# Every second attention head of the last two chunks in token-major form: normalized probabilities turned by the DMA crossbar, value-stationary products

## The chip, the core and the metric

The kernel runs on one core of one Trainium2 chip. Such a core has a matrix engine (TensorE, "PE" in the profile, with its weight loads as "PEld"), VectorE (DVE), ScalarE (ACT), GpSimd (POOL), SyncE (SP, which here only issues DMAs) and 16 DMA engines. Matrix products read SBUF and write PSUM, which has eight banks of 512 float32 columns. The metric is the device time of one execution in microseconds (us); lower is better.

## What is computed

A transformer block with 2048 tokens of width 1024, whose two halves are scaled, shifted and gated by six vectors made from a condition `c` (`mod = silu(c) @ w_mod`):

```python
h = layernorm(x) * (1 + ca) + sa
q = (h @ wq).reshape(2048, 32, 128)          # 32 query heads of width 128
k, v = last 512 cached keys and values        # 4 key/value heads, each for 8 query heads
p = softmax(q @ k.T * 128 ** -0.5)            # no mask: every token sees the same 512 keys
x = x + ga * ((p @ v) @ wo)
h = layernorm(x) * (1 + cb) + sb
x = x + gb * ((silu(h @ w_gate) * (h @ w_up)) @ w_down)     # inner width 3584
```

Inputs and output are bfloat16.

## The kernel before

**Chunks and heads.** The tokens are worked in 4 chunks of 512. The attention half is one loop over `i` from 1 to 129, where head number `i` counts all 4 x 32 heads (chunk `i // 32`, head `i % 32`). The loop is a software pipeline written out by hand. Iteration `i` issues, in this order: the query projection of head `i + 3` (`qproj`, L642: eight matmuls into PSUM bank 4, then a DVE cast into one of five `qT` slots), the scores of head `i - 1` (`scores`, L805) and the value products of head `i - 2` (`pv`, L816). When a chunk's last head is through, the output projection of that chunk follows (`oproj`, L872: eight groups of 32 matmuls, in banks 4 and 7, each ended by two DVE operations of `resid`, L851). In the last chunk it is spread over the end of the loop and the code behind it. Then comes the feed-forward half, chunk by chunk: `gateup` and `down`.

**One head.** `scores` is key-major: for each of four key tiles, the keys are the stationary operand and the 512 queries move, so that banks 0 to 3 hold scores with keys on partitions. Two ACT exponentials of 1024 columns each (L813) write them, not normalized, to `ex_s`. `pv` then needs no transposition for its products: for every token tile `j` and key tile `kt` the probabilities are stationary and the values move, with a column of ones appended, 129 columns in all (16 matmuls into banks 5 and 6). The ones give the sum of each token's row. DVE takes its reciprocal (L831), multiplies (L834) and a DMA transpose (L837) turns the result to the form that the output projection needs, `oT_all`.

**Queues.** Every operation goes through one tracker (`_Tracker.op`, L62), which puts waits on semaphores ahead of it in its engine's queue; each queue runs in program order. A wait of DVE for an earlier DVE result is a wait as well. All attention DMAs are issued from SP, so a DMA whose source isn't ready holds all later ones: the `oT` transposes, the 1 MB loads of `wq` for four heads each (`load_wq`, L353), the transposes of the next layernorm (L454), and 24 transposing loads of `w_mod` columns (`load_mt`, L584), each followed by a DVE operation with an accumulated sum (`mod_col`, L592).

**Side work.** `bg` holds generators for the layernorm of the next chunk; `run_bg(1)` at the end of each iteration takes one step of it (a half of the statistics, the rest of them, the normalization with its transpose, and at the end the modulation of two tiles). It is filled at the third iteration of a chunk and lasts 19 steps. `LOADT` gives the iterations of the 24 column loads, one every 9/4 heads from iteration 34 on, and `mod_col` follows four iterations behind its load. `wq` is loaded at iterations with `i % 4 == 1`; the load for group `(i + 4) // 4 + 1` of four heads is first used by the query projection four iterations later.

**Memory.** Nearly all of SBUF is one array, `arena`, in which regions are reused by offset; a new region inherits the waits of what it overlaps (`_Arena.at`, L103). `tmp` are the two scratch tiles of `resid`.

Of the kernel before, what the change touches and what calls it, by code (L numbers as in the profile page):

```python
# [3 lines left out]
ALU = mybir.AluOpType  # L4
AF = mybir.ActivationFunctionType
BF16 = mybir.dt.bfloat16
F32 = mybir.dt.float32
P = 128
# [122 lines left out]
def bass_adaLN_cond__sliding_block_cached__swiglu_ffn__prompt_kernel(  # L131
# [27 lines left out]
    TPC = CH // P  # L159
# [3 lines left out]
    att_scale = float(Dh) ** -0.5  # L163
    eps = 1e-5
    NA = NCH * Hq
# [29 lines left out]
    rstd = [rstd4[:, i:i + 1] for i in range(4)]  # L195
    bq = S_("bq", [P, 8], F32)
    rl = [S_("rl%d" % i, [P, 4], F32) for i in range(2)]
    nsc = [S_("nsc%d" % i, [P, D], BF16) for i in range(2)]
    tmp = [S_("tmp%d" % i, [P, 512], F32) for i in range(2)]

    KB = 1024
    A_BYTES = 162 * KB
    arena_t = S_("arena", [P, A_BYTES // 2], BF16)
    arena = _Arena(arena_t[:, :], A_BYTES)
# [6 lines left out]
    OFF_H20 = 154 * KB  # L211
# [10 lines left out]
    def bank(b, n=512, off=0):  # L222
        return ps[:, b * 512 + off:b * 512 + off + n]
# [10 lines left out]
    PB = [_Buf("bank%d" % b) for b in range(8)]  # L234
# [8 lines left out]
    B_mv = [_Buf("mv%d" % i) for i in range(4)]  # L243
    B_rs = [_Buf("rs%d" % i) for i in range(4)]
    B_rl = [_Buf("rl%d" % i) for i in range(2)]
    B_ns = [_Buf("ns%d" % i) for i in range(2)]
    B_tmp = [_Buf("tmp%d" % i) for i in range(2)]
    B_h2 = [[_Buf("h2_%d_%d" % (s, dt)) for dt in range(DT)] for s in range(2)]
# [8 lines left out]
    SCB = 0  # L257
    PVB = 5
    XB = 7

    with nc.Block() as block:

        @block.gpsimd
        def _(g):
            V = nc.vector
            A = nc.scalar
            TE = nc.tensor
            SP = nc.sync

            def mm(out_ap, lhsT, rhs, start, stop, reads, bank_buf, skip=False):  # L270
                T.op(PE, lambda: TE.matmul(out_ap, lhsT, rhs, start=start, stop=stop, skip_group_check=skip),  # L271
                     reads=reads, writes=[bank_buf])
# [7 lines left out]
            def run_bg(n=1):  # L280
                while n > 0 and bg:
                    try:
                        next(bg[0])
                        n -= 1
                    except StopIteration:
                        bg.pop(0)

            def finish(gen):
                while gen in bg:
# [6 lines left out]
                 reads=[B_ident], writes=[B_ident])  # L296
# [17 lines left out]
            OFF_HT = 80 * KB  # L314
            OFF_OT = 96 * KB
            OFF_EX = 128 * KB
# [56 lines left out]
            B_va = _Buf("va")  # L373
# [254 lines left out]
            def q_slot(i):  # L628
                return NQT + i % 2 if i < NQ0 else i % NQT
# [186 lines left out]
            def pv(i):  # L816
                ch, h = divmod(i, Hq)
                gk = h // rep
                es = i % NEX
                os_ = i % NOS  # L820

                for jj in range(2):
                    for kt in range(KT):
                        for jb in range(2):
                            j = 2 * jb + jj
                            b = PVB + jb
                            mm(bank(b, P + 1, jj * 130), ex_s[es][:, kt, j * P:(j + 1) * P], v_aug[:, gk * KT + kt, 0:P + 1],
                               kt == 0, kt == KT - 1, [B_ex[es], B_va, B_vg[gk]], PB[b])
                both = [PB[PVB], PB[PVB + 1]]
                r = i % 2  # L830
                T.op(DVE, lambda: V.reciprocal(rl[r][:, :].rearrange("p (a b) -> p a b", a=2), psap(PVB * 512 + P, [[512, 2], [130, 2]])),  # L831
                     writes=both + [B_rl[r]])
                rlb = bass.AP(tensor=rl[r][:, :].tensor, offset=0, ap=[[4, P], [2, 2], [1, 2], [0, P]])
                T.op(DVE, lambda: V.tensor_tensor(o_s[os_].rearrange("p (a b) d -> p a b d", a=2),  # L834
                                                  psap(PVB * 512, [[512, 2], [130, 2], [1, P]]), rlb, ALU.mult),
                     reads=[B_rl[r]], writes=both + [B_os[os_]])
                T.op(Q_tr[os_], lambda: SP.dma_start_transpose(oT_all[:, h, :].rearrange("p (j q) -> p j q", j=TPC),  # L837
                                                               o_s[os_].rearrange("p j d -> p (j d)")),
                     reads=[B_os[os_]], writes=[B_oT[h]])

            B_wo = [_Buf("wo%d" % i) for i in range(8)]
            wo_s = [None] * 8
            Q_wo = [dq("q_wo%d" % i) for i in range(8)]
# [49 lines left out]
            GATER = {19 + n: NGP + n for n in range(DT - NGP)}  # L893
            GATET = {23: 0, 24: 1}
            GATES = {26: 0, 27: 1}
            t2 = Hq + 6 + (9 * (NL - 1)) // 4
            TURNT = (28, t2 + 1)
            PUTT = {33: (0, c_sil, B_csil), 30: (1, mrow[0:DT, :], B_mrow), t2 + 3: (2, mrow[0:DT, :], B_mrow)}
            GETT = {35: (0, sc_row, B_scr), 31: (1, rowb[0][:, :], B_row[0]), t2 + 4: (2, rowb[1][:, :], B_row[1])}
            LOADT = {Hq + 2 + (9 * n) // 4: n for n in range(NL)}  # L900
            LOADO = {5 + (21 * p) // 8: p for p in range(8)}
            LOADK = {1: 1, 5: 2, 6: 3}
            for i in range(1, NA + 2):
                ch, h = divmod(i, Hq)
                if i in LOADK:
                    load_k(LOADK[i])
                if i == 4:
                    load_wq((i + 4) // 4 + 1)
# [24 lines left out]
                if i + LEAD < NA:  # L933
                    if (i + LEAD) % Hq == 0:
                        finish(ln1[(i + LEAD) // Hq])
                    if i == 1:
                        scores(0)
                    if i in (1, 3, 5):
                        q_bias_mm(i + 1, i + 3, XB)
                    if i > NQ0:  # L940
                        qproj(i + LEAD)
                    elif i % 2 == 1:
                        qproj_mm(NQ0 + i // 2, QB, 0, HK)
                    else:
                        qproj(NQ0 - 1 + i // 2, QB, HK)
                if i - 4 in LOADT:
                    n = LOADT[i - 4]
                    mod_col(n)
                    g0, last = divmod(n, DT)
                    if last == DT - 1:  # L950
                        mod_take(g0, B_late[g0 + 1])
                        if g0 == 1:
                            mod_gain(1, B_late[2], B_g[1])
                n = i - (NA - LEAD)
                if 0 <= n <= 2:
                    oproj_mm(NCH - 1, 0, QB, 8 * n, 8 * n + 8)
                elif n >= 3:
                    oproj_mm(NCH - 1, 1, XB, 8 * (n - 3), 8 * (n - 3) + 8)
                if 1 <= i - 1 < NA:
                    scores(i - 1)  # L960
                if 0 <= i - 2 < NA:
                    pv(i - 2)
                    ch2, h2 = divmod(i - 2, Hq)
                    if i % 4 == 1 and i > 5:
                        load_wq((i + 4) // 4 + 1)
                    if i in LOADT:
                        load_mt(LOADT[i])
                    if h2 == Hq - 1 and ch2 < NCH - 1:
                        oproj(ch2)
                run_bg(1)  # L970
                for n in GATEP.get(i, ()):
                    gate_part(n)
                if i in GATER:
                    gate_row(GATER[i])
                if i in GATES:
                    gate_sum(GATES[i])
                if i == max(GATER):
                    gate_split()
# [152 lines left out]
```

## Time and profile before

| what | value |
|---|---|
| median of 3 runs | 1270.15 us (1269.91 to 1270.49) |
| the profiled execution's own time | 1270.14 us |
| its span, from the first to the last instruction | 1268.3 us |
| granted TensorE clock | 1.00 |
| attention of chunk 2 (iterations 66 to 97, from the trace) | about 361 to 472 us |
| attention of chunk 3 | about 528 to 638 us |
| busy in the stretch 359 to 470 us: PE, DVE, ACT | 110.16, 72.21, 63.43 of 111 us |
| busy in the stretch 526 to 637 us: PE, DVE, ACT | 110.16, 57.08, 63.43 of 111 us |

The span is what the trace shows; 1.8 us of the execution lie around it. A busy share of PE is the union of its matmul records, whose ends are modelled, so it tells that something was always in flight and not how fast; the pace is read from the distance between events that follow a fixed number of matmuls. SP is a queue that issues DMAs: its instruction's duration is the issue, and the data land later ("to landing", counted from the start of the issue).

### The profile page before, as it was taken

The page shows a single profiled execution, that of the slowest core. Times are in us where ns is not written, and L with a number is a line of the kernel's source. Part 1 is how long each engine was busy: PE and PEld are TensorE (multiplying, and loading weights), DVE is VectorE, ACT ScalarE, POOL GpSimd, SP SyncE. Part 2 cuts the span into 40 slices and gives each one's busy share as a digit, 9 for nine tenths or more (in the row PEclk, how much of TensorE's full clock was granted, in tenths as well). Part 3 has the DMA queues.
Part 4 walks back from the last instruction along what each step waited for, and adds up shares of the span by engine and source line. Part 5 has one row for each costly group of instructions (what it writes and reads, how often), then busy time and mean ns, then how long its engine had stood idle before and what let it go on. Part 6 is the DMA issues. An engine that isn't in the chain of part 4 may idle for free.

```text
span 1268.3 us, 17609 instructions
## 1 busy us (share of the span) xinstructions
PE 1255.1 (99%) x7442; PEld 640.7 (51%) x7583; DVE 485.1 (38%) x894; ACT 341.6 (27%) x389; POOL 56.0 (4%) x95
## 2 busy tenths in 40 slices
PE   8999999999999999999999999999999999999999
PEld 5655545555455554555544444444444444444444
DVE  4676226764257641365322321233212321222122
ACT  4655205553035550155510111011100111011100
POOL 1530000000000000000000000000000000000000
PEclk9999999999999999999999999999999999999999
DMA  9998306875029641064243972055512644034200
GB/s 320 264 263 218 92 1 127 177 171 125 1 57 177 138 114 34 9 129 123 61 145 100 291 246 94 25 158 150 168 40 72 177 141 134 17 128 154 67 9 25
DMA packets 239997, 156.67 MB, mean 124 GB/s; under 512 B 133296, under 2 KB 225840, under 8 KB 239920
## 3 DMA queue, kind: packets, MB, share of 16 engines
q1 hardware_dynamic: 181664, 96.83, 31.6%
q10 hardware_dynamic: 58256, 58.73, 14.6%
q8 instruction: 59, 0.97, 0.3%
q14 instruction: 18, 0.15, 0.1%
HBM read 119.93 MB, written 4.20 MB: 98 GB/s over the span
## 4 chain that ended last, share of the span: by engine, by line
PE 98%; issue 1%; DMA 0%; SPq 0%; DVE 0%
PE ps L271 98%; DMA arena<-in_w_mod_dram 0%; SPq L309 0%; SPq L334 0%; PE ps L275 0%; DVE arena L496 0%; DVE tmp L853 0%; DVE arena L855 0%; DVE gain_f L486 0%
## 5 line engine op out<-in xcount | busy, mean ns | idle before, releaser
L271 PE MATMUL ps<-arena 128*128 128x512 bf16 (+1 forms) x7213 | 1249.3, 333 | 10.1 <-POOL arena L298 2.0
L271 PEld LDWEIGHTS ps<-arena 128*128 128x128 bf16 x7354 | 632.9, 98 | 621.5 <-issue 2.1
L813 ACT ACTIVATE arena<-ps 128x1024 bf16<-128x1024 f32 x256 | 261.9, 1023 | 345.1 <-PE ps L271 333.4
L1059 ACT ACTIVATE arena<-ps 128x512 bf16<-128x512 f32 x112 | 66.9, 597 | 499.6 <-PE ps L271 499.6
L1060 DVE TENSOR_TENSOR arena<-ps,arena 128x512 bf16<-128x512 f32 x112 | 77.5, 692 | 276.2 <-PE ps L271 276.2
L853 DVE TENSOR_TENSOR tmp<-ps,rowb 128x512 f32<-128x512 f32 (+1 forms) x65 | 44.4, 683 | 318.8 <-PE ps L271 318.8
L644 DVE CAST arena<-ps 128x512 bf16<-128x512 f32 x120 | 82.8, 690 | 47.7 <-PE ps L271 47.7
L834 DVE TENSOR_TENSOR arena<-ps,rl 128x512 bf16<-128x512 f32 x128 | 88.5, 691 | 4.7 <-DVE rl L831 0.2
L831 DVE RECIPROCAL rl<-ps 128x4 f32<-128x4 f32 x128 | 23.4, 182 | 114.1 <-PE ps L271 114.1
L429 POOL TENSOR_SCALAR rstd<-mv 128x1 f32<-128x1 f32 x28 | 6.1, 216 | 910.3 <-DVE mv L428 910.3
L424 DVE BATCH_NORM_STATS2 st<-x_res 128x6 f32<-128x512 bf16 x62 | 42.4, 683 | 3.4 <-DMA x_res<-in_A_x_dram 3.3
L593 DVE SCALAR_TENSOR_TENSOR arena<-arena 128x1024 bf16<-128x1024 bf16 x24 | 29.2, 1215 | 0.0
L855 DVE TENSOR_TENSOR arena<-tmp,x_res 128x512 bf16<-128x512 f32 (+2 forms) x33 | 22.3, 677 | 1.1
L855 DVE TENSOR_TENSOR x_res<-tmp,x_res 128x512 bf16<-128x512 f32 x32 | 22.2, 693 | 1.1
L440 DVE TENSOR_SCALAR arena<-arena,gain,mod_bf 128x512 bf16<-128x512 bf16 x56 | 21.2, 420 | 0.0
L435 DVE TENSOR_SCALAR nsc<-x_res,mv,rstd 128x1024 bf16<-128x1024 bf16 x30 | 19.2, 641 | 0.0
L431 POOL TENSOR_TENSOR rstd<-rstd,mhalf 128x1 f32<-128x1 f32 x28 | 15.7, 559 | 2.3
L772 POOL TENSOR_SCALAR arena<-arena,sc_bf 128x512 f32<-128x512 bf16 x8 | 12.9, 1614 | 0.5 <-POOL arena L774 0.2
L774 POOL TENSOR_TENSOR arena<-arena 128x512 f32<-128x512 f32 x8 | 10.1, 1265 | 0.7
L428 DVE BATCH_NORM_AGGREGATE mv<-st 128x2 f32<-128x12 f32 x28 | 5.8, 209 | 1.0
L271 PEld LDWEIGHTS ps<-sc_bf,arena 128*128 128x128 bf16 x128 | 4.4, 96 | 1.4 <-DMA arena<-in_w_mod_dram 0.3
L271 PE MATMUL ps<-sc_bf,arena 128*128 128x1 bf16 x128 | 4.7, 164 | 0.3 <-DMA arena<-in_w_mod_dram 0.3
(56 smaller groups left out, 59.4 us busy)
## 6 DMA issues: line engine op xcount, KB each, us to landing
arena<-in_A_wq_dram SPq DMA_DIRECT2D x30, 1024.0 KB, 5.8
arena<-in_B_w_gate_dram ACTq DMA_DIRECT2D x28, 1024.0 KB, 5.4
arena<-in_B_w_up_dram ACTq DMA_DIRECT2D x28, 1024.0 KB, 7.9
arena<-in_A_wo_dram SPq DMA_DIRECT2D x8, 1024.0 KB, 7.6
arena<-in_B_w_down_dram SPq DMA_DIRECT2D x7, 1024.0 KB, 8.3
out_dram<-arena SPq DMA_DIRECT2D x15, 256.0 KB, 2.0
x_res<-in_A_x_dram SPq DMA_DIRECT2D x3, 1024.0 KB, 7.0
arena<-arena SPq DMA_TRANSPOSE x132, 2.6
```

The costliest lines, as they stand in the source:

```text
L271: T.op(PE, lambda: TE.matmul(out_ap, lhsT, rhs, start=start, stop=stop, skip_group_check=skip), reads=reads, writes=[bank_buf])
L424: T.op(DVE, lambda: V.bn_stats(st_[sl][:, hf * 6:hf * 6 + 6], x_res[:, t, hf * 512:hf * 512 + 512]), reads=[B_x[t]], writes=[B_st[sl]])
L440: T.op(DVE, lambda: V.tensor_scalar(dst[:, dt, :], dst[:, dt, :], gain[gi][:, dt:dt + 1], mod_bf[:, ccol + dt:ccol + dt + 1], op0=ALU.mult ...
L593: T.op(DVE, lambda: V.scalar_tensor_tensor(mt[n % 2], mt[n % 2], 1.0, sc_row, op0=ALU.mult, op1=ALU.mult, accum_out=mcol[:, n:n + 1]), rea ...
L644: T.op(DVE, lambda: V.tensor_copy(qT_s[qs], bank(b)), writes=[PB[b], B_qT[qs]])
L813: T.op(ACT, lambda: A.activation(ex_s[es][:, 2 * kp:2 * kp + 2, :], banks2(SCB + 2 * kp), AF.Exp, scale=att_scale), writes=[PB[SCB + 2 * k ...
L831: T.op(DVE, lambda: V.reciprocal(rl[r][:, :].rearrange("p (a b) -> p a b", a=2), psap(PVB * 512 + P, [[512, 2], [130, 2]])), writes=both + ...
L834: T.op(DVE, lambda: V.tensor_tensor(o_s[os_].rearrange("p (a b) d -> p a b d", a=2), psap(PVB * 512, [[512, 2], [130, 2], [1, P]]), rlb, A ...
L853: T.op(DVE, lambda: V.tensor_tensor(tmp[s][:, 0:n], bank(b, n), rowb[ri][:, c0:c0 + n], ALU.mult), reads=[B_row[ri]], writes=[PB[b], B_tmp ...
L855: T.op(DVE, lambda: V.tensor_tensor(dst[:, c0:c0 + n], tmp[s][:, 0:n], x_res[:, t, c0:c0 + n], ALU.add), reads=[B_tmp[s], B_x[t]], writes= ...
L1059: T.op(ACT, lambda: A.activation(sg_s[ss], bank(gb), AF.Silu), writes=[PB[gb], B_sg[ss]])
L1060: T.op(DVE, lambda: V.tensor_tensor(guT[:, ft, :], bank(ub), sg_s[ss], ALU.mult), reads=[B_sg[ss]], writes=[PB[ub], B_gu[ft]])
```

## The change

The 31 heads 66, 68, ..., 126 (`NAT`: the even ones of chunks 2 and 3, without head 64) go another way.

- **Scores token-major** (`nat_scores`): for each of four token tiles the queries are stationary and the 512 keys move, still four matmuls of 512 columns in banks 0 to 3, but with tokens on partitions. Four ACT exponentials of 512 columns, each with an accumulated row sum (`psum`), write `pn`. They are issued two iterations earlier in the count of heads than `scores` would be: in the odd iteration `i`, for head `i + 1`, between the query projection and the value products.
- **Normalization** (`nat_norm`), in two halves of two token tiles: a DVE reciprocal of two sums, then two DVE multiplications of 512 columns in place. The first half is issued in the odd iteration behind `pv(i - 2)`, the second in the next one behind its query cast.
- **Turning** (`nat_turn`): each half, 128 x 1024 values, goes through a DMA transpose of SP to `pt`, so that keys are on partitions.
- **Products** (`nat_pv`), three iterations behind the scores: four matmuls with the values stationary and 512 tokens moving, into bank 5. The result is already in the form of `oT_all`; one DVE copy puts it there, without a DMA.
- **Room.** `pn` of even slots takes the place of one `ex_s`, that of odd slots the two `tmp`; `pt` (two slots of 4 KB a partition) moves through three regions that are free at the time (`PTAT`).
- **Seams.** Where a chunk ends (iterations 65 and 97) the early scores come behind `pv`, and the two transposes behind the output projection.
- **Moved with it.** `wq` is loaded at `i % 4 == 2` from iteration 66 on, so one iteration later. The 24 column loads come every 3/2 heads instead of 9/4, `mod_col` three iterations behind its load instead of four, and the last row's turning and loading follow earlier. `run_bg(1)` comes ahead of the early scores in odd iterations.

```diff
+            NAT = set(range(2 * Hq + 2, NA, 2))
+            B_pn = [[_Buf("pn0_%d" % hf) for hf in range(2)], B_tmp]
+            pn = [[None, None], [t[:, :].bitcast(BF16) for t in tmp]]
...
+            def nat_scores(i):
...
+                for j in range(TPC):
+                    mm(bank(SCB + j), qT_s[qs][:, j * P:(j + 1) * P],
+                       kT_sb[:, gk * KT:(gk + 1) * KT, :].rearrange("p a b -> p (a b)"), True, True,
+                       [B_kT[gk], B_qT[qs]], PB[SCB + j])
+                for j in range(TPC):
+                    hf, jj = divmod(j, 2)
+                    T.op(ACT, lambda: A.activation(pn[s][hf][:, jj * 512:(jj + 1) * 512], bank(SCB + j), AF.Exp, scale=att_scale,
+                                                   accum_out=psum[s][:, j:j + 1]),
+                         writes=[PB[SCB + j], B_pn[s][hf], B_psum[s][hf]])
+
+            def nat_norm(i, hf):
+                s = p_slot(i)
+                T.op(DVE, lambda: V.reciprocal(pinv[s][:, 2 * hf:2 * hf + 2], psum[s][:, 2 * hf:2 * hf + 2]),
+                     reads=[B_psum[s][hf]], writes=[B_pinv[s][hf]])
+                for jj in range(2):
+                    j = 2 * hf + jj
+                    T.op(DVE, lambda: V.tensor_scalar(pn[s][hf][:, jj * 512:(jj + 1) * 512], pn[s][hf][:, jj * 512:(jj + 1) * 512],
+                                                      pinv[s][:, j:j + 1], None, op0=ALU.mult),
+                         reads=[B_pinv[s][hf]], writes=[B_pn[s][hf]])
+
+            def nat_turn(i, hf):
+                s = p_slot(i)
+                pt_of[i] = (pt[s], B_pt[s])
+                T.op(Q_pt[2 * s + hf], lambda: SP.dma_start_transpose(pt[s][:, 2 * KT * hf:2 * KT * (hf + 1), :], pn[s][hf]),
+                     reads=[B_pn[s][hf]], writes=[B_pt[s][hf]])
+
+            def nat_pv(i):
...
+                for kt in range(KT):
+                    mm(bank(PVB).rearrange("p (j q) -> p j q", j=TPC), v_aug[:, gk * KT + kt, 0:P], ptv[:, :, kt, :],
+                       kt == 0, kt == KT - 1, [B_va, B_vg[gk]] + pb, PB[PVB])
+                T.op(DVE, lambda: V.tensor_copy(oT_all[:, h, :], bank(PVB)), writes=[PB[PVB], B_oT[h]])
...
-            LOADT = {Hq + 2 + (9 * n) // 4: n for n in range(NL)}
+            LOADT = {Hq + 2 + (3 * n) // 2: n for n in range(NL)}
...
+            PTAT = {2 * Hq + 2: OFF_OT + 24 * KB, 2 * Hq + 16: OFF_H20, 3 * Hq: OFF_HT}
...
+                seam = (i - 1) % Hq == 0 and i + 1 in NAT
+                if i + 1 in PTAT and not seam:
+                    pt_region(PTAT[i + 1])
+                if i in NAT and (i - 2) % Hq:
+                    nat_norm(i, 1)
+                    nat_turn(i, 1)
+                nat = i % 2 == 1 and i + 1 in NAT
+                if nat and not seam:
+                    run_bg(1)
+                    nat_scores(i + 1)
-                if 1 <= i - 1 < NA:
+                if 1 <= i - 1 < NA and i - 1 not in NAT:
                     scores(i - 1)
                 if 0 <= i - 2 < NA:
-                    pv(i - 2)
+                    if i - 2 in NAT:
+                        nat_pv(i - 2)
+                    else:
+                        pv(i - 2)
+                    if nat:
+                        if seam:
+                            nat_scores(i + 1)
+                        nat_norm(i + 1, 0)
+                        if seam:
+                            nat_norm(i + 1, 1)
+                        else:
+                            nat_turn(i + 1, 0)
                     ch2, h2 = divmod(i - 2, Hq)
-                    if i % 4 == 1 and i > 5:
+                    if i % 4 == (1 if i < 2 * Hq else 2) and i > 5:
                         load_wq((i + 4) // 4 + 1)
```

More of the change, by code (lines that the diff above doesn't have):

```diff
@@ L197, in bass_adaLN_cond__sliding_block_cached__swiglu_ffn__prompt_kernel @@
     rl = [S_("rl%d" % i, [P, 4], F32) for i in range(2)]
+    psum = [S_("psum%d" % i, [P, 4], F32) for i in range(2)]
+    pinv = [S_("pinv%d" % i, [P, 4], F32) for i in range(2)]
     nsc = [S_("nsc%d" % i, [P, D], BF16) for i in range(2)]
@@ L245, in bass_adaLN_cond__sliding_block_cached__swiglu_ffn__prompt_kernel @@
     B_rl = [_Buf("rl%d" % i) for i in range(2)]
+    B_psum = [[_Buf("psum%d_%d" % (i, hf)) for hf in range(2)] for i in range(2)]
+    B_pinv = [[_Buf("pinv%d_%d" % (i, hf)) for hf in range(2)] for i in range(2)]
     B_ns = [_Buf("ns%d" % i) for i in range(2)]
@@ L839, in pv, with p_slot @@
                      reads=[B_os[os_]], writes=[B_oT[h]])
+            NAT = set(range(2 * Hq + 2, NA, 2))
+            B_pn = [[_Buf("pn0_%d" % hf) for hf in range(2)], B_tmp]
+            pn = [[None, None], [t[:, :].bitcast(BF16) for t in tmp]]
+            B_pt = [[_Buf("pt%d_%d" % (s, hf)) for hf in range(2)] for s in range(2)]
+            pt = [None, None]
+            pt_of = {}
+            Q_pt = [dq("q_pt%d" % i) for i in range(4)]
+            def p_slot(i):
+                return (i - (2 * Hq + 2)) // 2 % 2
@@ new lines, in pt_region @@
+            def pt_region(off):
+                for s in range(2):
+                    old = B_pt[s]
+                    B_pt[s] = [_Buf("pt%d_%d" % (s, hf)) for hf in range(2)]
+                    for hf in range(2):
+                        B_pt[s][hf].absorb(old[hf])
+                    pt[s] = arena.at(off + s * 4 * KB, [TPC * KT, P], BF16, B_pt[s])
+            def nat_scores(i):
+                gk = i % Hq // rep
+                qs = q_slot(i)
+                s = p_slot(i)
+                if pn[0][0] is None:
+                    for hf in range(2):
+                        pn[0][hf] = arena.at(OFF_EX + hf * 2 * KB, [2 * KT * P], BF16, [B_pn[0][hf]])
+                for j in range(TPC):
[7 more added lines that the diff above has]
+                         writes=[PB[SCB + j], B_pn[s][hf], B_psum[s][hf]])
@@ new lines, in nat_turn @@
+            def nat_turn(i, hf):
+                s = p_slot(i)
+                pt_of[i] = (pt[s], B_pt[s])
+                T.op(Q_pt[2 * s + hf], lambda: SP.dma_start_transpose(pt[s][:, 2 * KT * hf:2 * KT * (hf + 1), :], pn[s][hf]),
+                     reads=[B_pn[s][hf]], writes=[B_pt[s][hf]])
+            def nat_pv(i):
+                h = i % Hq
+                gk = h // rep
+                s = p_slot(i)
+                pa, pb = pt_of.pop(i)
+                ptv = pa.rearrange("p (j k) q -> p j k q", j=TPC)
+                for kt in range(KT):
+                    mm(bank(PVB).rearrange("p (j q) -> p j q", j=TPC), v_aug[:, gk * KT + kt, 0:P], ptv[:, :, kt, :],
+                       kt == 0, kt == KT - 1, [B_va, B_vg[gk]] + pb, PB[PVB])
+                T.op(DVE, lambda: V.tensor_copy(oT_all[:, h, :], bank(PVB)), writes=[PB[PVB], B_oT[h]])
@@ L895, in _ @@
             GATES = {26: 0, 27: 1}
-            t2 = Hq + 6 + (9 * (NL - 1)) // 4
+            t2 = Hq + 6 + (3 * (NL - 1)) // 2
             TURNT = (28, t2 + 1)
@@ L945, in _ @@
                         qproj(NQ0 - 1 + i // 2, QB, HK)
-                if i - 4 in LOADT:
-                    n = LOADT[i - 4]
+                if i - 3 in LOADT:
+                    n = LOADT[i - 3]
                     mod_col(n)
@@ L969, in _ @@
                         oproj(ch2)
-                run_bg(1)
+                        if seam:
+                            if i + 1 in PTAT:
+                                pt_region(PTAT[i + 1])
+                            for hf in range(2):
+                                nat_turn(i + 1, hf)
+                if not nat or seam:
+                    run_bg(1)
                 for n in GATEP.get(i, ()):
```

## The prediction

> **What bounds the kernel now.** I read the page first: the busy shares, then the chain that ended last, then the groups with their shapes kept apart.
>
> ```profile
> PE 1255.1 (99%) x7442; PEld 640.7 (51%) x7583; DVE 485.1 (38%) x894; ACT 341.6 (27%) x389; POOL 56.0 (4%) x95
> ...
> PE 98%; issue 1%; DMA 0%; SPq 0%; DVE 0%
> ...
> L271 PE MATMUL ps<-arena 128*128 128x512 bf16 x5085 | 1134.2, 380 | 9.5 <-POOL arena L298 2.0
> ...
> L271 PE MATMUL ps<-arena 128*128 128x129 bf16 x2048 | 137.0, 220 | 0.0
> ```
>
> PE is the path nearly everywhere, and in the attention of chunks 2 and 3 the list of waits shows none of PE. So only two things count: how many slots PE needs, and whether something new makes it wait. The matmul records overlap, so their means are no prices. I take the pace from the timeline: gate-up work first (16 matmuls of 512 columns from one SiLU on ACT, L1059, to the next), then four heads of chunk 3, then the landings of the wq loads (L357) of chunks 2 and 3.
>
> ```profile
> 700.83 0.60 ACT L1059 ACTIVATE arena<-ps 128x512 bf16<-128x512 f32 x1 [2.86 <-PE ps L271]
> 707.73 0.60 ACT L1059 ACTIVATE arena<-ps 128x512 bf16<-128x512 f32 x1 [2.86 <-PE ps L271]
> ```
> ```profile
> 547.28 2.14 ACT L813 ACTIVATE arena<-ps 128x1024 bf16<-128x1024 f32 x2 [1.36 <-PE ps L271]
> 548.62 0.18 DVE L831 RECIPROCAL rl<-ps 128x4 f32<-128x4 f32 x1 [1.08 <-PE ps L271]
> 548.84 0.69 DVE L834 TENSOR_TENSOR arena<-ps,rl 128x512 bf16<-128x512 f32 x1
> 549.44 0.54 DVE L435 TENSOR_SCALAR nsc<-x_res,mv,rstd 128x1024 bf16<-128x1024 bf16 x1
> 550.35 0.69 DVE L644 CAST arena<-ps 128x512 bf16<-128x512 f32 x1 [0.36 <-PE ps L271]
> ...
> 557.77 2.14 ACT L813 ACTIVATE arena<-ps 128x1024 bf16<-128x1024 f32 x2 [1.36 <-PE ps L271]
> 557.83 0.53 SPq L357 DMA_DIRECT2D arena<-in_A_wq_dram  x1
> ```
> ```profile
> L357 SPq DMA_DIRECT2D arena<-in_A_wq_dram x13: 506/532/535, 376.7 to 599.8; - x13
> ...
> DMA to landing us min/median/max: 5.3/5.8/7.5
> ```
>
> From 700.83 to 707.73 lie 32 matmuls: 0.2156 us each. From 547.28 to 557.77 lie three heads: 3.497 each. A head has 12 matmuls of 512 columns (2.587), so its 16 of 129 columns take 0.910, or 0.057 each. A wq load of those two chunks lands 5.3 to 7.5 us after its issue. The last matmul's record outlasts its slot by 0.16 (0.380 less 0.216), and at the kernel's end DVE starts 0.04 behind it; so an engine sees a product 0.2 after PE's slot has passed on.
>
> **The change, part by part.** *Products.* Sixteen slots (0.910) become four (0.862): 0.048 less, 31 times, **-1.5 us**. The new moving operand is read in four runs of 128 columns; no row has that. If each run paid the 0.057 of a 129-column slot, the four matmuls would take 0.912 and the gain were nothing; below 0.862 there is no row. I take 0.862, the row of the same 512 columns. The scores keep four slots.
>
> The Trainium skill ("TensorE: Matmul & The Clock Gate", section "Back-to-back issue gap") gives sustained spacings of about 81 ns at 128 columns and 131 ns at 512. By it, as an estimate, a head would save 16 x 0.081 - 4 x 0.131 = 0.77 and the change 24 us. The trace disagrees on both, 57 and 216 ns, and decides.
>
> *ACT.* Two exponentials (2.14) become four of 512 columns: 0.60 each by L1059's row, plus 0.19 for reading the accumulator (L518's row) and up to 0.09, the pause between the two of a head; 3.1 to 3.5 together. A pair of heads then has 5.3 to 5.6 of 6.95 us. It lies beside PE as long as bank 3 is free for the next scores. The odd iteration taken as zero, in times that engines see: query products 1.73, early scores 1.94 to 2.59, value products 3.50; then 5.22, scores 6.08, new products 6.95. The four exponentials run from 1.94 to 5.1 or 5.4; PE's slot for bank 3 comes at 6.08 - 0.22 - 0.2 = 5.66. Covered; if one cost 0.93 instead, the cover is gone, and each us more is paid once a pair.
>
> *DVE.* Reciprocal and multiplication (0.9) become two reciprocals (0.21 each up to the next start), four multiplications of 0.35 (L675, one scalar) to 0.41 (L440, two) and a copy of 0.69. Per pair, with two layernorm steps of about 0.75, some 6.4 of 6.95. The first half can start behind L834: 3.50 + 0.22 + 0.61 (next starts 0.60 behind it above) = 4.33, and lasts 0.21 + 0.35 + 0.04 + 0.35 = 0.95, to 5.28. The cast holds DVE to 5.89, the second half ends at 6.84 (7.07 with the dearer row). Bank 4 is free a us ahead of the next query products. Cover enough.
>
> *The turned halves.* Each is shaped like a layernorm transpose (L454: issue 1.25, landing 3.1, median 3.7, 6.2 at most in these chunks). The second goes out at 6.87 and is read at 13.03 - 0.2: 5.9 us. Hidden; only a landing near 6.2 would show. The `oT` transpose (landing 2.4 to 2.7 mostly) goes away; the copy replaces it in time.
>
> *The wq load.* This is where I see a wait. Before, SP issued it behind the odd head's `oT` transpose, 5.71 into its iteration (557.83 against 552.12), four iterations ahead of its use: 4 x 3.497 - 0.2 - 5.71 = 8.1 us for a landing of 7.5 at most. Now it stands behind the second turn, which stands behind DVE: 6.87 + 1.25 + 0.09 = 8.21, that is 4.71 into the even iteration, and three iterations ahead: 3.449 + 3.497 + 3.449 - 0.2 - 4.71 = **5.5 us**. Median landing 5.8 and a PE restart of some 0.1 make 0.4; with the dearer multiplication 0.6. Ends: nothing (5.3) and 2.0 (7.5). I take 0.45, nearest to the median, as the quiet landings (5.4 to 5.6) are of loads with fewer transposes around. Loads of iterations 74 to 94 and 102 to 118 are so placed, 11; that of 98 isn't, as SP waits for nothing at that seam. **+5.0** (0 to 22).
>
> *Start of chunk 2.* (a) In iteration 65 the early scores follow scores 64 by one `pv` (0.91): bank 2 is wanted 0.91 + 0.43 - 0.2 = 1.14 behind the end of those scores, and the second exponential ends 1.71 behind it (2.14 less 0.43): **+0.6**. Iteration 97 has no scores ahead: nothing. (b) The load for heads 72 to 75 went out ahead of the output projection; now its turn comes behind the turns of head 66, which wait for that projection's end (their room is `oT`), and behind the `oT` of head 64: 5.7 into iteration 66 by the timeline (first `oT` issue of the chunk 4.4 behind the projection's end). Left: 10.44 - 0.2 - 5.7 = 4.5 against 5.8: **+1.3** (0.8 to 3.0). (c) `mod_col` (1.21) runs in iterations 67, 68, 70 and 71, in the same queue ahead of the normalization. The load of iteration 70 is so issued 1.2 later than in a quiet pair: 0.4 + 1.2 = **+1.5** (0.5 to 3).
>
> *The other moves.* The denser column loads put 1.21 on DVE in two of three iterations of chunk 1: with cast, reciprocal, multiplication and a layernorm step 3.0 of 3.50; landings of 3.1 to 6.4 against three heads. Issue on SP (1.3 to 2.4) fits between the `oT`. Regions of `pt` are free before they are entered (last `mod_col` in 71, room entered in 79; `hT` of chunk 2 last read in 92). `tmp` under `pn` delays `resid` at seam 97 only if a turn hadn't landed in the 6.9 us of the first group. Nothing; if DVE overflowed, bank 4 would pass it on one to one.
>
> **Sum.** -1.5 + 0.6 + 1.3 + 1.5 + 5.0 = +6.9. Span 1268.3 to 1275.2; the profiled execution took 1270.14, the median of the runs shown is 1270.15, so **1277.0**.
>
> **Rivals.**
> - *The wq load is hidden* (not slower): SP gets to it early or landings stay at 5.3 to 5.5. For: five of the 13 loads land within 5.6. Against: 5.5 leaves no room, and a 256 KB turn runs just ahead. It decides at 5.4. With (b) and (c) halved by the same: -1.5 + 0.6 + 1.4 = +0.5: 1270.7.
> - *SP becomes late*: a third transpose in a row is issued slowly. For: the one at 395.59, third in a row, took 2.24 instead of 1.25. Against: a wq load was in flight there, and in the pair of the load none is. One us more for each load: +18: 1288.
> - *ACT holds bank 3*: exponentials with a sum at 1.05 each instead of 0.8 to 0.88, 0.5 over in each of 31 pairs: +22 with the rest: 1292. L518's 1.06 for 1024 columns with a sum, against 1.02 without, speaks against it.
> - *The gain isn't there* (strided operand): +1.5 on the forecast, 1278.5, within its range.
> - *129-column products are bound by their weight loads* (record 0.098 each), so that 16 loads become 4: faster, 1246. The pace of 0.057 excludes it nearly. The skill's page above would have it so.
>
> **How the numbers follow.** Chances: forecast with its variant 0.64, hidden 0.22, SP 0.08, ACT 0.05, weight loads 0.01. The predicted time is the forecast's. Range: from the hidden case to the forecast with 0.9 per load and the upper ends of (b) and (c): 1270.2 to 1285.0; SP's and ACT's cases stay out. A difference under 0.2% (2.5 us) can hardly be told from none here: hidden (0.19 of its 0.22) and a forecast with a tenth of a us per load (0.03) fall within it; faster: 0.02, the weight loads and a hidden case with no start-up loss. Slower: 0.76.
>
> **What would show it.** Right: PE waits in chunks 2 and 3 released by DMA `arena<-in_A_wq_dram`, about 13 of them, 0.3 to 1.5 us each; one on ACT at the seam; the distance of two pairs 13.9 us plus one such wait. L357 issued behind a turn, some 4.7 us into its iteration. Wrong: PE waits named after transposes from `tmp` or `arena`, after ACT in every pair, or after DVE (the cast); pairs shorter than 6.9 us; or no waits at all. I'd be wrong mostly by the landing of wq behind a turn, which no row shows.

## The result, and the profile after

The changed kernel took **1288.4 us** (median of 5 runs, 1287.08 to 1292.74) against 1270.15: 1.0149 times the time before, 95% interval 1.0130 to 1.0167. The profiled execution took 1288.4 us with a span of 1286.6, so the span grew by 18.3 us.

The page of the changed kernel: busy shares, then the chain that ended last, by engine and by line.

```profile
PE 1256.3 (98%) x7076; PEld 623.8 (48%) x7211; DVE 526.9 (41%) x1049; ACT 360.1 (28%) x575; POOL 56.0 (4%) x95
...
PE 88%; DMA 7%; DVE 3%; issue 1%; SPq 1%; ACT 0%
```

PE's busy share fell by one point only, but the chain tells more: 7% of it are now DMA, where it had none before. The waits of PE, first in a stretch that holds chunk 1, then in two that hold chunks 2 and 3 (total us, how often, longest us):

```profile
PE ps L275 <- DVE arena L838: 1.0, 1, 1.0
PE ps L275 <- DVE rl L835: 0.5, 1, 0.5
PE ps L275 <- ACT arena L817: 0.5, 1, 0.5
PE ps L275 <- DVE arena L648: 0.3, 1, 0.3
```
```profile
PE ps L275 <- DMA arena<-in_A_wq_dram: 7.5, 7, 1.5
PE ps L275 <- DVE st L428: 2.1, 1, 2.1
PE ps L275 <- issue: 0.5, 1, 0.5
```
```profile
PE ps L275 <- DMA arena<-in_A_wq_dram: 5.4, 5, 2.2
```

The kernel before had no wait in any of the three. The one put down to DVE (L428, 2.1 us at 392.05) falls on the query projection that first uses the wq load issued at 385.24 and landed 6.5 us later, and the weight load ahead of it (at 391.82) is put down to wq, so it belongs to wq too: 13 such waits. A gap counts from the modelled end of the last matmul, which lies 0.17 us behind its slot. On three of the 13 (392.05, 467.44, 566.76) PE's first record comes 0.23 us behind the weight load, elsewhere 0.01: there a matmul's record is missing, and the gap reads a slot (0.22) too long. So the slots lost to wq are 13.0 + 2.1 - 3 x 0.22 + 13 x 0.17 = 16.7 us.

The wait called "issue" (0.55 us at 413.31) is another matter. PE's next work there is the new products of a turned head: their copy (L906, 414.37) starts 1.06 us later, which is four matmuls and the lag of 0.2. The turned half was issued at 407.98, behind the load of the last modulation row (L621), and landed 5.2 us later. With the end of the record this wait costs 0.7.

One pair of heads with a load, from the timeline of the changed kernel (start, duration, engine and line; some lines left out at the marks):

```profile
424.56 0.69 DVE L648 CAST arena<-ps 128x512 bf16<-128x512 f32 x1 [2.55 <-PE ps L275]
424.77 0.60 ACT L877 ACTIVATE arena<-ps 128x512 bf16<-128x512 f32 x1 [2.61 <-PE ps L275]
...
425.26 0.20 ACT L877 ACTIVATION_READ_ACCUMULATOR arena<-ps 128x1 f32 x1
...
426.33 0.18 DVE L835 RECIPROCAL rl<-ps 128x4 f32<-128x4 f32 x1 [0.43 <-PE ps L275]
...
427.26 1.19 SPq L841 DMA_TRANSPOSE arena<-arena  x1
427.34 0.74 DVE L887 TENSOR_SCALAR arena<-arena,pinv 128x512 bf16<-128x512 bf16 x2
...
428.55 2.64 SPq L894 DMA_TRANSPOSE arena<-arena  x2
428.66 0.16 DVE L883 RECIPROCAL pinv<-psum 128x2 f32<-128x2 f32 x1
428.85 0.74 DVE L887 TENSOR_SCALAR arena<-arena,pinv 128x512 bf16<-128x512 bf16 x2
...
431.28 0.53 SPq L361 DMA_DIRECT2D arena<-in_A_wq_dram  x1
...
437.87 2.33 PE L275 MATMUL ps<-arena 128*128 128x512 bf16 x9 [1.18 <-DMA arena<-in_A_wq_dram]
```

The odd iteration begins at 424.56 - 1.73 = 422.83, the even one at 426.33. SP works off three transposes without a pause, 427.26 to 431.19, and then issues the wq load, 4.95 us into the even iteration. It lands 6.5 us later and PE goes on at once. DVE is done with the second half at 429.59 and its turn is issued at 429.9, so SP, not DVE, sets the load's place by then, though by 0.3 us only.

### The profile page after: what moved, and what is told of

Same layout as the page of the kernel before. It is cut to its first block, busy times and chain, and to the rows that moved or that the text cites. A ratio compares the mean times of both kernels' runs of the same rounds, so it can differ in the third digit from the quotient of the medians.

```text
span 1286.6 us, 17348 instructions
## 1 busy us (share of the span) xinstructions
PE 1256.3 (98%) x7076; PEld 623.8 (48%) x7211; DVE 526.9 (41%) x1049; ACT 360.1 (28%) x575; POOL 56.0 (4%) x95
## 4 chain that ended last, share of the span: by engine, by line
PE 88%; DMA 7%; DVE 3%; issue 1%; SPq 1%; ACT 0%
PE ps L275 88%; DMA arena<-in_A_wq_dram 6%; DMA arena<-in_w_mod_dram 1%; DVE st L428 1%; DVE arena L906 1%; SPq L894 1%; DVE arena L838 0%; DVE arena L648 0%; DVE arena L597 0%; DMA x_res<-in_A_x_dram 0%; DVE nsc L439 0%; PE ps L279 0%; DVE tmp L887 0%; DVE arena L887 0%; DVE rl L835 0%
## 5 line engine op out<-in xcount | busy, mean ns | idle before, releaser
L275 PEld LDWEIGHTS ps<-arena 128*128 128x128 bf16 x6982 | 616.2, 98 | 656.8 <-DMA arena<-in_A_wq_dram 20.8
L817 ACT ACTIVATE arena<-ps 128x1024 bf16<-128x1024 f32 x194 | 198.5, 1023 | 288.2 <-PE ps L275 279.3
L1154 ACT ACTIVATE arena<-ps 128x512 bf16<-128x512 f32 x112 | 66.9, 597 | 500.2 <-PE ps L275 500.2
L648 DVE CAST arena<-ps 128x512 bf16<-128x512 f32 x120 | 82.7, 689 | 55.3 <-PE ps L275 55.3
L838 DVE TENSOR_TENSOR arena<-ps,rl 128x512 bf16<-128x512 f32 x97 | 67.1, 691 | 3.4
L877 ACT ACTIVATE arena<-ps 128x512 bf16<-128x512 f32 x64 | 37.9, 595 | 37.4 <-PE ps L275 30.8
L835 DVE RECIPROCAL rl<-ps 128x4 f32<-128x4 f32 x97 | 17.6, 181 | 68.1 <-PE ps L275 68.1
L428 DVE BATCH_NORM_STATS2 st<-x_res 128x6 f32<-128x512 bf16 x62 | 42.4, 683 | 3.5 <-DMA x_res<-in_A_x_dram 3.4
L877 ACT ACTIVATE tmp<-ps 128x512 bf16<-128x512 f32 x60 | 35.5, 595 | 20.0 <-PE ps L275 17.2
L906 DVE CAST arena<-ps 128x512 bf16<-128x512 f32 x31 | 21.4, 691 | 9.8 <-PE ps L275 9.8
L887 DVE TENSOR_SCALAR arena<-arena,pinv 128x512 bf16<-128x512 bf16 x64 | 22.6, 353 | 2.3
L887 DVE TENSOR_SCALAR tmp<-tmp,pinv 128x512 bf16<-128x512 bf16 x60 | 21.2, 353 | 2.1
```

The lines of the kernel that those rows point to most:

```text
L428: T.op(DVE, lambda: V.bn_stats(st_[sl][:, hf * 6:hf * 6 + 6], x_res[:, t, hf * 512:hf * 512 + 512]), reads=[B_x[t]], writes=[B_st[sl]])
L648: T.op(DVE, lambda: V.tensor_copy(qT_s[qs], bank(b)), writes=[PB[b], B_qT[qs]])
L817: T.op(ACT, lambda: A.activation(ex_s[es][:, 2 * kp:2 * kp + 2, :], banks2(SCB + 2 * kp), AF.Exp, scale=att_scale), writes=[PB[SCB + 2 * k ...
L877: T.op(ACT, lambda: A.activation(pn[s][hf][:, jj * 512:(jj + 1) * 512], bank(SCB + j), AF.Exp, scale=att_scale, accum_out=psum[s][:, j:j + ...
L887: T.op(DVE, lambda: V.tensor_scalar(pn[s][hf][:, jj * 512:(jj + 1) * 512], pn[s][hf][:, jj * 512:(jj + 1) * 512], pinv[s][:, j:j + 1], Non ...
L906: T.op(DVE, lambda: V.tensor_copy(oT_all[:, h, :], bank(PVB)), writes=[PB[PVB], B_oT[h]])
```

## The experiments

Ratios are to the kernel before, with 95% intervals; its median was 1270.3 to 1270.6 in these comparisons.

**1. The load two iterations earlier.**

```diff
-                    if i % 4 == (1 if i < 2 * Hq else 2) and i > 5:
+                    if i % 4 == (1 if i < 2 * Hq else 0) and i > 5:
```

> The changed kernel with one edit: from head count 64 on, wq is loaded at i % 4 == 0 instead of 2, so two iterations earlier. Theory A (PE's new waits are for wq alone, because its load is asked for 4.95 us into an even iteration and lands 6.2 us later against 5.2 us that are left): the deadline moves out by about 6.95 us, all 13 waits go, 17.3 us with them: 1288.4 to about 1271. PE waits for in_A_wq_dram none in chunks 2 and 3. Theory B (SP or the DMA engines are too full with the turned halves; the load is only the first to feel it): the waits reappear on the turned halves or on the casts and the time stays above 1280.

1278.3 us, ratio 1.0062 (1.0047 to 1.0077): 10 us less than the change, not 17. PE's gaps of this run, from the timeline of PE alone from chunk 1 to the end of attention:

```profile
237.02 70.54 PE L275 MATMUL ps<-arena 128*128 128x512 bf16 x562 [0.32 <-DVE arena L648]
308.02 79.44 PE L275 MATMUL ps<-arena 128*128 128x512 bf16 x414 [0.46 <-ACT arena L817]
390.66 22.46 PE L275 MATMUL ps<-arena 128*128 128x512 bf16 x132 [3.20 <-DMA arena<-arena]
413.55 7.11 PE L275 MATMUL ps<-arena 128*128 128x512 bf16 x44 [0.43 <-issue]
421.97 238.23 PE L275 MATMUL ps<-arena 128*128 128x512 bf16 x1398 [1.31 <-issue]
```

No wait for wq is left, as theory A said, and from 422 us on PE runs without a gap through the rest of chunk 2 and all of chunk 3, with 26 turned heads. But theory B holds for the beginning of chunk 2: three waits, the first named after a transpose within `arena`, a turned half; the other two end when the turned halves land that were issued at 407.85 and in the pair of turns from 415.78 on. In the changed kernel only the second of them shows (the 0.55 us at 413.31); the others were hidden behind the waits for wq. Behind the first wait the granted clock falls as well, to 0.78 and 0.80 in the two stretches of 4 us from 388 us on: three pairs of heads, 132 records, take 22.46 us there, where three pairs at 6.95 and the end of a record make 21.0. The count closes: -1.3 for the products, 0.6 at the seam, 1.6 in chunk 1, 5.4 for the three waits, 1.4 for the clock: +7.7, and the span is 7.8 longer than before. The waits for wq that went were worth 16.7; waits and clock at the start of chunk 2 took 6.1 more than in the change.

**2. The load one iteration earlier.**

```diff
-                    if i % 4 == (1 if i < 2 * Hq else 2) and i > 5:
+                    if i % 4 == 1 and i > 5:
```

> The changed kernel with wq loaded at i % 4 == 1 throughout, as in the kernel before: in the odd iteration, behind the first turned half and ahead of the second. Theory A: asked for about 7.1 us into an odd iteration, 13.9 - 0.2 - 7.1 = 6.6 us are left for a landing of about 6.2: waits of 0 to 0.5 us, about 1272 to 1276. But the second half of that pair now lies behind 1 MB: it goes out at about 6.9 to 7.7 us and must have landed at 12.8; a landing of 5 to 6 us as in the layernorm transposes behind a load would show as a few PE waits for it, up to 0.8 us for each of 13 loads. Theory B: above 1280 all the same.

1300.15 us, ratio 1.0229 (1.0214 to 1.0245): worse than the change itself. In chunks 2 and 3 the waits for wq are gone and 14 others of 21.6 us in all have come. One of them, in the timeline:

```profile
464.70 0.57 SPq L361 DMA_DIRECT2D arena<-in_A_wq_dram  x1
465.37 2.78 SPq L894 DMA_TRANSPOSE arena<-arena  x1
...
471.90 13.41 PE L275 MATMUL ps<-arena 128*128 128x512 bf16 x85 [1.23 <-issue]
472.96 0.69 DVE L906 CAST arena<-ps 128x512 bf16<-128x512 f32 x1 [1.57 <-PE ps L275]
```

The second half is now issued right behind 1 MB; its issue alone takes 2.78 us instead of 1.3, and PE stands still until 471.90. What it does then is the new products: their copy (L906) starts 1.06 us later, four matmuls and the lag of 0.2. So it waited for the turned half, which landed 6.4 us after its issue. I had expected up to 0.8 for each; it was 1.7 with the ends of the records.

**3. The moved load alone, without any turned head.** In the kernel before:

```diff
-                    if i % 4 == 1 and i > 5:
+                    if i % 4 == (1 if i < 2 * Hq else 2) and i > 5:
```

> The kernel before with one edit taken from the change: from head count 64 on, wq is loaded at i % 4 == 2 instead of 1. No head is turned. Theory A: asked for 5.71 us into its iteration with three iterations of 3.497 us left, 10.49 - 0.2 - 5.71 = 4.58 us against a landing of about 5.8: 1.25 us for each of 14 loads, +17.5 us: about 1287.6, so nearly what the whole change costs. Theory B: SP and the DMA engines are no fuller than before, so 1270 to 1275.

1294.4 us, ratio 1.0191 (1.0168 to 1.0214). One line, with nothing else of the change, costs 24 us, more than the whole change. The waits of PE in chunks 2 and 3:

```profile
PE ps L271 <- DMA arena<-in_A_wq_dram: 17.1, 14, 2.3
```

With the ends of the records that is 19.4 us, 1.39 each (expected 1.25). The rest of the 22.8 us by which this span is longer is the clock, below.

**4. The denser column loads alone**, in the kernel before:

```diff
-            LOADT = {Hq + 2 + (9 * n) // 4: n for n in range(NL)}
+            LOADT = {Hq + 2 + (3 * n) // 2: n for n in range(NL)}
...
-                if i - 4 in LOADT:
-                    n = LOADT[i - 4]
+                if i - 3 in LOADT:
+                    n = LOADT[i - 3]
```

> The kernel before with the other moved part alone: the 24 column loads every 3/2 heads instead of 9/4 and used three iterations later instead of four. In the changed kernel DVE waits 3.8 us for two of them in chunk 1 and PE then about 1.8 us for DVE. If that comes from the spacing alone: +1.5 to +2, about 1272, and the same two waits near 221 to 237 us. If it needs the rest of the change (it comes 70 us ahead of the first turned head): no difference, 1270.2.

1271.55 us, ratio 1.0009 (0.9999 to 1.0018): 1.2 us more, with the interval just touching one. The waits of PE and of DVE in chunk 1 are there without any turned head:

```profile
PE ps L271 <- DVE arena L834: 0.4, 1, 0.4
PE ps L271 <- DVE arena L644: 0.3, 1, 0.3
```
```profile
DVE arena L593 <- DMA arena<-in_w_mod_dram: 2.5, 2, 1.9
```

**5. Is the load of x among them the cause?** As 1, with

```diff
-            LOADX = {19: 2, 40: 3}
+            LOADX = {19: 2, 55: 3}
```

> As wq_two_earlier, and the 1 MB load of x for the last chunk moved from iteration 40 to 55. Theory: the wait of DVE for two late column loads in chunk 1 (then of PE for DVE, 1.5 us with the ends of the records) comes from that load lying among the denser column loads: it goes, 1278.3 to about 1276.8. Rival: the column loads are late by themselves (every fourth one behind a wq load), the wait stays within 0.3 us or comes up elsewhere in chunk 1. The waits for turned halves near 390 to 422 us should stay.

1277.55 us (1275.81 to 1278.36), ratio 1.0050 (1.0035 to 1.0065), within the spread of experiment 1. PE still waits 0.18, 0.42 and 0.54 us at the same places (1.6 for chunk 1 in experiment 1, 1.6 now, both with the ends of the records). The load of x is not the cause; by experiment 4 the spacing is enough. The waits for turned halves stay as expected (3.4, 0.3 and 1.6 us).

**6. Turned heads from 80 on.** As 1, with the first turned head behind the column loads and most of the layernorm of chunk 2:

```diff
-            NAT = set(range(2 * Hq + 2, NA, 2))
+            NAT = set(range(2 * Hq + 16, NA, 2))
...
-            PTAT = {2 * Hq + 2: OFF_OT + 24 * KB, 2 * Hq + 16: OFF_H20, 3 * Hq: OFF_HT}
+            PTAT = {2 * Hq + 16: OFF_H20, 3 * Hq: OFF_HT}
...
+                first = i + 1 == min(NAT)
+                if i in NAT and (i - 2) % Hq and i != min(NAT):
...
+                        if first:
+                            for hf in range(2):
+                                nat_turn(i + 1, hf)
```

> As wq_two_earlier, but the first turned head is 80 instead of 66, so 24 heads instead of 31; its scores follow the value products as at a seam. Column loads and most of the layernorm transposes of chunk 2 then lie ahead of the first turned half. Theory: the waits for turned halves near 390 to 422 us (4.9 us, and 1.7 us of slower TensorE clock behind them) come from these DMAs sharing SP's queue with the turns: none is left, and the seam wait stays: -1.2 + 0.6 + 1.5 = +0.9 on the kernel before: about 1271.2. Rival: the turned halves don't fit into chunk 2 with wq loads at all: waits of PE for them stay, and the time is above 1274.

1274.4 us, ratio 1.0030 (1.0019 to 1.0041): the three waits near 390 to 422 us are gone. That fits the theory, though it doesn't prove it, since the turned heads of that place are gone too. The time is 3 us above what I expected. Two new waits, 2.1 us with the ends of the records, make most of it, chunk 1 (0.7 more) and a second gap at the first turned head (0.28 us) the rest. The first of the two is:

```profile
306.52 0.54 SPq L361 DMA_DIRECT2D arena<-in_A_wq_dram  x1
...
309.77 1.30 SPq L841 DMA_TRANSPOSE arena<-arena  x1
```
```profile
315.53 98.12 PE L275 MATMUL ps<-arena 128*128 128x512 bf16 x607 [1.08 <-DMA arena<-arena]
```

The load of iteration 64 stands ahead of the `oT` transpose of the last head of chunk 1, which lands 5.7 us after its issue at 309.77, and the output projection wants it in its first group of 32 matmuls. Experiment 1 has no such wait; there the early scores and the wait for their bank at the seam come first. The second (0.64 us at 557.14) lies in chunk 3 and is one for a turned half again: the copy of the new products (L906, 558.20) starts 1.06 us later. Its turn stands behind a wq load (545.01) and a layernorm transpose whose issue takes 2.25 us. So even with this early load one of the turned halves comes late.

**7.** The same with x loaded at 55.

> As early_from_head_80, and the load of x for the last chunk moved from iteration 40 to 55. Theory: nothing waits but the one bank wait at the first turned head: -1.2 + 0.6 = -0.6 on the kernel before, 1269.7, not to be told from it. If the products' gain of 0.048 us a head isn't there, 1270.9.

1273.74 us (10 runs), ratio 1.0027 (1.0018 to 1.0036): 4 us above the expectation, with the two waits of 6 somewhat shorter (0.80 and 0.51 us); span 1271.6. The first of them carries a warning: a load that is early enough for its user has become a load that is in another's way.

**8. The load ahead of the second half, in the same iteration**, as in the change otherwise:

```diff
                     nat_norm(i, 1)
+                    if i % 4 == 2 and i > 2 * Hq + 2:
+                        load_wq((i + 4) // 4 + 1)
                     nat_turn(i, 1)
...
-                    if i % 4 == (1 if i < 2 * Hq else 2) and i > 5:
+                    if i % 4 == (1 if i < 2 * Hq else 2) and i > 5 and not (i in NAT and i > 2 * Hq + 2 and (i - 2) % Hq):
```

> The changed kernel with the wq load in the same even iteration as there, but ahead of the second turned half instead of behind it (from iteration 70 on). Theory (what lies first in SP's queue lands in time, what lies second is late): wq is asked for about 3.6 us into the iteration, 6.6 us left for 6.1: its waits shrink from 1.2 to 0 to 0.3 us. The turned half goes out at about 4.3 to 4.5 us into the iteration, behind 1 MB, and lands 6.5 us later as in wq_one_earlier: 10.9 against 9.3: 1.5 us of wait for 12 loads, now ahead of the new products: 1288 to 1294, no better than the change. If instead the turned half lands in 3 to 5 us: about 1275.

1302.15 us, ratio 1.0234 (1.0214 to 1.0254), the slowest of all. In the profiled run the clock drops three times, behind the waits of 3.15, 2.28 and 3.30 us, and the records behind them take 6.3 us longer in all; the waits themselves, 14 of 23.2 us, are dearer than expected too. A stretch of the timeline:

```profile
435.44 0.53 SPq L361 DMA_DIRECT2D arena<-in_A_wq_dram  x1
436.06 2.82 SPq L894 DMA_TRANSPOSE arena<-arena  x1
```
```profile
443.54 14.06 PE L275 MATMUL ps<-arena 128*128 128x512 bf16 x88 [2.17 <-issue]
```

The turned half landed 7.4 us after its issue, and the new products start then (their copy follows at 444.61). The only wait for wq that is left is that of the load of iteration 66, which this edit doesn't move. With these deadlines, whichever of the two comes second in the queue is late.

**9. An attempt at a version without waits**: 20 turned heads, from 88 on (built as in 6), the column loads every 2 heads and four iterations ahead of their use, and the load at `i % 4 == 0` except at the seam:

```diff
+            LOADT = {Hq + 2 + 2 * n: n for n in range(NL)}
...
+                    if (i == 3 * Hq + 2 or i % 4 == (1 if i < 2 * Hq + 24 else 0) and i != 3 * Hq) and i > 5:
```

> An attempt at a version without waits: 20 turned heads from 88 on, the column loads every 2 heads with four iterations to their use (done before head 88), wq at i % 4 == 0 from iteration 88 on except at the seam, where it is asked for at 98. Theory: -0.8 to -1.0 for the products, +0.6 for the bank wait at the first turned head, 0 to +0.6 for the denser column loads: 1270.0 to 1270.6, not to be told from the kernel before. A time above 1272 would mean that the turned halves or the denser loads still hold something up.

1270.45 us (11 runs) against 1270.43, ratio 1.0000 (0.9992 to 1.0009). All of PE's gaps from 100 to 700 us:

```profile
99.70 338.17 PE L275 MATMUL ps<-arena 128*128 128x512 bf16 x2333
438.33 4.10 PE L275 MATMUL ps<-arena 128*128 128x512 bf16 x30 [0.46 <-ACT arena L817]
442.72 13.20 PE L275 MATMUL ps<-arena 128*128 128x512 bf16 x84 [0.28 <-DVE rl L835]
456.14 244.23 PE L275 MATMUL ps<-arena 128*128 128x512 bf16 x1355 [0.23 <-issue]
```

Three gaps, 1.5 us with the ends of the records, eat the 0.9 that 20 heads save. Two are at the first turned head. The third, at 456.14, is a turned half once more: the copy of the products (L906, 457.20) starts 1.06 us later, and a turn issued behind the wq load of 445.29 took 6.5 us to land. No version here beats the kernel before.

## Why the prediction was wrong, point by point

The direction and the mechanism were forecast, the size was not: +6.9 us against +18.3, outside the range. The terms, by the changed kernel's trace (the products by the pace of experiment 1):

| step | forecast | measured |
|---|---|---|
| products | -1.5 | -1.3 |
| seam, (a) | +0.6 | +0.6 |
| load of iteration 66, (b) | +1.3 | +1.6 |
| load of iteration 70, (c) | +1.5 | +2.1 |
| 11 later wq loads | +5.0 | +13.0 |
| turned halves | 0 | +0.7 |
| other moves (column loads) | 0 | about +2 |

The measured terms add up to 18.7, against 18.3.

- *Products.* Two heads take 6.950 us where nothing waits (experiment 1: exponentials of the odd heads at 574.29 and 636.84, nine pairs), against 6.993 before (571.76 to 634.70, 18 heads). The saving is 0.043 for a turned head, so the strided operand costs nothing that shows. The weight-load rival and the page's spacings behind it are out.
- *ACT and DVE* came as worked out. The rows of the new operations, shapes kept apart:

```profile
L877 ACT ACTIVATE arena<-ps 128x512 bf16<-128x512 f32 x64 | 37.9, 595 | 37.4 <-PE ps L275 30.8 <-DVE rl L835 3.7
L887 DVE TENSOR_SCALAR arena<-arena,pinv 128x512 bf16<-128x512 bf16 x64 | 22.6, 353 | 2.3
...
L877 ACT ACTIVATION_READ_ACCUMULATOR arena<-ps 128x1 f32 x64 | 12.6, 196 | 0.0
```

  0.595 + 0.196 for an exponential with its sum, 0.353 for a multiplication; the one wait for a bank in chunks 2 and 3 is at the seam. ACT's rival is out.
- *The wq load*, the step that failed. It was named with its place, its cause and its formula; the term was mis-sized. I took 0.45 for each of the 11 loads, the range went up to 0.9, and a load costs 1.18 (11 gaps of 11.5 us, two of them a slot too long, with 0.17 each). Three things went into that. First, I put the median landing into a formula in which every landing above the deadline costs. The 13 landings of the kernel before are 6.1 us in the mean, not 5.8, with four from 6.9 to 7.5; load by load the same formula would have given 0.7. Second, the load is issued later: 4.9 to 5.0 into the iteration instead of 4.71 for eight of the loads, 5.7 to 5.8 for three, of which two stand behind a pair of turns that took 3.4 to 3.5 us to issue instead of 2.6 and one behind a layernorm transpose. Third, the landings with turned halves around are longer: in chunks 2 and 3 of the changed kernel 5.8 at least, 6.1 in the median and 6.2 in the mean; experiment 3, with the load in the same iteration and no turned halves, has 5.6 in the median and experiment 1, with turned halves, 6.2. I had named that risk and then sized the term by loads without one.
- *The other moves.* "Nothing" was wrong by about 2 us in the change and 1.2 alone (experiment 4). I compared the landing of one column load with three heads; where the denser loads queue up with wq and x, DVE waits 3.8 us for two of them, and bank 4 and the value banks pass on part of it. Chunk 1 has no turned head, and three of the kernels with the same code there (the change, experiments 1 and 6) lose between 1.6 and 2.3 us in it; why it cost less in experiment 4 is not settled.
- *Turned halves hidden.* True in steady state, and in chunk 3 of experiment 1 throughout, but not at the start of chunk 2, and not for single halves behind a wq load (experiments 6, 7 and 9). In the change one wait of 0.7 us shows and the rest was covered by the waits for wq. That is why undoing the late load gave back 10 us and not 17.
- *The rivals.* "Hidden" is out. "SP becomes late" gave about the right time, 1288, but not the right way: the turns of the changed kernel take 1.3 us to issue in the median, and a pair of them was slow (3.4 to 3.5 us) ahead of two of the 11 loads only. That the time matches is chance. Turned halves right behind a 1 MB load take 2.3 to 2.9 (experiments 2 and 8).

Of the code one more thing. At iteration 65 the early exponentials of head 66 go into the `ex_s` slot whose probabilities of head 64 are read only in iteration 66. The tracker knows only of reads already issued, so it puts no wait there, and by the order of the code the products of head 64 in chunk 2 are made from head 66's values: the changed kernel computes this head wrongly, and so do experiments 1, 2, 5 and 8. In experiments 6, 7 and 9 the first turned head uses the other slot. A version with the wait that is missing was not run, so what it would cost at the seam is open.

## What to carry to other kernels

Moving a load by one iteration is an edit with a price of its own: compare issue to deadline with all the landings in the new surroundings, not with the median in the old, and add up every landing that misses. In one DMA queue what comes second pays for what comes first, so an added transfer has to be counted against every deadline behind it. And when one late transfer is mended, look for the next that it covered before promising its whole cost back.

## What the hardware showed that I had not expected

Waits cost more than their own length. In experiment 3 the wait at 419.80 lasted 2.2 us, and the clock granted to TensorE fell behind it (stretch, its length, PE busy and records, granted clock, DMA share, GB/s):

```profile
419.80 15.75 PE L271 MATMUL ps<-arena 128*128 128x512 bf16 x112 [2.19 <-DMA arena<-in_A_wq_dram]
```
```profile
416.00:420.00 4.00, 1.81 (x21) 0.95 1.41 226
420.00:424.00 4.00, 4.00 (x13) 0.62 0.29 64
```

The same 112 records take 15.75 us there and 14.16 behind the shorter waits: 1.6 us on top. It came again behind the wait of 2.0 us at 582.91, but not behind that of 2.28 at 601.03; the changed kernel's profiled run, with a wait of 2.2, shows none. In chunks 2 and 3 of all the profiles there are 14 gaps of 2.0 us or more (counted as the profile reads them, without the one whose record is missing). Eight were followed by a slower clock, the shortest of them 2.00 us long, and six were not, the longest of them 2.76. The Trainium skill ("TensorE: Matmul & The Clock Gate", section "HAM oscillation — how this bites in real kernels") puts the bound at gaps above about 3.4 us. Here 2.0 us between records, some 2.2 between slots, was enough at times, and the granted clock of a 4 us stretch behind such a wait was 0.62 in the lines above and 0.50 at the lowest (experiment 8, from 392 us). It may explain the wide spread of the changed kernel's runs, whose mean clock lies between 0.997 and 1.000; that was not tested.
